# Loads of v and token weights spread over batch 0's attention in a fused attention and two-mixer kernel

## The chip, the cores and the metric

The kernel runs on one core of one Trainium2 chip. The metric is the device time of one execution in microseconds (us); the kernel before takes 465.46 us, the median of three runs (464.9 to 465.52).

The core's engines run their own instruction streams and meet at semaphores: TensorE (PE, and PEld for its weight loads), VectorE (DVE), ScalarE (ACT), GpSimd (POOL) and SyncE (SP), which here issues every transfer between HBM and the on-chip memory.

## The reference

Three stages follow one another, with batch 2, sequence 768 and width 512 (8 heads of 64):

```python
k_sum = k.reshape(B, H, nb, 32, D).max(axis=3)       # block maxima of the keys, nb = 24
v_sum = v.reshape(B, H, nb, 32, D).mean(axis=3)      # block means of the values
scores_l = where(|i - j| < 16, q @ k.T / 8, -1e9)    # a band of 31 keys
scores_s = q @ k_sum.T / 8 + log(32)                 # the 24 blocks
x = softmax([scores_l, scores_s]) @ [v, v_sum]
h = relu(x.T @ w_tok1) @ w_tok2;   u = x + h.T       # token mixing, 768 -> 256 -> 768
x = u + relu(u @ w_ch1) @ w_ch2                      # channel mixing, 512 -> 1536 -> 512
xk, xr = mu * x + (1 - mu) * x_prev                  # time shift, twice
out = sigmoid(xr @ w_r) * (relu(xk @ w_k)**2 @ w_v)
```

All inputs and the output are float32.

## The kernel before

Attention works on 12 query tiles of 128 rows, 0 to 5 for batch 0 and 6 to 11 for batch 1. For tile u the steps are named `sc` (scores: banded products of 32 queries with 64 keys, the block maxima beside them, and at the end two products that add the mask, lines 298 and 304), `max` (maximum and subtraction on DVE), `en` and `ef` (exponentials on ACT), `tr` and `tc` (transposes on PE, copied out by ACT), `pv` (products with the block means, line 348, and with v, line 355), `norm` (DVE, lines 365 and 366), then `xh` and `xl`, which split the result into a high and a low float32r part, since each large product is done as three (lines 191 to 193).

v comes in as one tile `vw` per query tile, with overlapping windows of 64 rows; `vu` (POOL, lines 247 to 250) copies the windows that overlap from neighbours. The block means of v are sums on PE: `vs b w` (line 272) multiplies window w of batch b by a constant and adds it into `vs[b]`; there are 13 windows in each batch, and the sums are complete with the last. `vd` then copies them to `vbd` on ACT (line 279), which the first `pv` needs. `km` takes the block maxima of the keys on DVE (line 254).

The token weights t1 and t2 come in three pieces each (`ld`). A piece is 64 bit words and is turned into float32 by `ca` (ACT, line 395) and `cj` (DVE, lines 407 and 408), then split by `ch` (ACT, 412) and `cl` (DVE, 415). `t1` is the first token product; `t1h` and `t1l` take its rectified high and low parts, h; `t2` is the second token product. It begins with transposes of x into the same accumulators (line 497).

The order of everything is written out by hand: `PLAN` (line 45) is a list of some 1,700 steps, and each engine runs its own instructions in that order. All transfers go out on SP in that order too. A step `gq`, `gv`, `gk`, `gx` or `gu` is a gate: SP copies one element of a tile to a scratch row (line 196), so that it, and every transfer behind it, waits until that tile has been written. 48 buffers of 4 KB a partition (`slot`) hold nearly all tiles; a new tile takes a buffer whose last reader is done.

Of the kernel before, what the change touches and what calls it, by code (L numbers as in the profile page):

```python
# [44 lines left out]
PLAN = """heat 6,vz 0,vz 1,lk 0 0,lk 0 1,km 0 0,lq 0 0 0,lk 0 2,km 0 1,lk 0 3,lq 0 0 1,km 0 2,msk,lq 0 1,cst,km 0 3,sc 0,pad 0,max 0  # L45
gq 0 0,lq 0 2,lv 0,sc 1,en 0,gq 0 1,lv 1,lv 2,ef 0,pad 1,max 1,sc 2,en 1,ef 1,gq 0 2,lv 3,lv 4,pad 2,max 2,sc 3,tr 0 0,gv 0
lv 5,ld t1 0,gv 2,ld t1 1,gv 4,ld t1 2,en 2,tc 0 0,ef 2,pad 3,max 3,tr 0 1,sc 4,tc 0 1,en 3,vs 0 0,vs 0 1,ef 3,tr 1 0,pad 4
max 4,vs 0 2,vs 0 3,tc 1 0,pad 5,vu 0,vu 1,tr 1 1,sc 5,tc 1 1,en 4,vs 0 4,vs 0 5,tr 2 0,ef 4,max 5,vs 0 6,vs 0 7,ca t1 0
tc 2 0,vu 2,vu 3,vs 0 8,vs 0 9,tr 2 1,ca t1 1,vs 0 10,tc 2 1,vs 0 11,vs 0 12,cj t1 0,tr 3 0,tr 3 1,vd 0,vu 4,vu 5,gv 5
ld t2 0,tc 3 0,pv 0,cj t1 1,tc 3 1,ch t1 0,ld t2 1,ca t1 2,cl t1 0,pv 1,norm 0,xh 0,cj t1 2,en 5,tr 4 0,ef 5,ld t2 2,xl 0  # L50
pv 2,norm 1,tc 4 0,tr 4 1,xh 1,t1 0,xl 1,pv 3,ch t1 1,norm 2,tc 4 1,mu,cl t1 1,gx 1,xh 2,norm 3,tr 5 0,gx 2,lk 1 0,t1 1,xl 2
tc 5 0,tr 5 1,ch t1 2,pv 4,tc 5 1,xh 3,gx 3,lk 1 1,cl t1 2,xl 3,pv 5,t1 2,ca t2 0,lk 1 2,norm 4,cj t2 0,ca t2 1,xh 4,ca t2 2
norm 5,xl 4,gk 1 0,lk 1 3,ch t2 0,gk 1 1,lv 6,cl t2 0,t1 3,gk 1 2,lv 7,xh 5,cj t2 1,t1 4,gk 1 3,lv 8,xl 5,ch t2 1,cj t2 2
vs 1 0,vs 1 1,t1 5,gv 6,lv 9,cl t2 1,ch t2 2,vs 1 2,om,vs 1 3,t1h 0 0,cl t2 2,gv 7,vu 6,lv 10,t1h 0 1,vs 1 4,vs 1 5,t1l 0 0
t1l 0 1,gv 8,vu 7,lv 11,km 1 0,vs 1 6,t2 0 0 0,km 1 1,gv 9,vu 8,ld c 0 0,km 1 2,t2 0 1 0,t2h 0 0 0,km 1 3,gv 10,vu 9,ld c 1 0
t2l 0 0 0,vs 1 7,vs 1 8,t2h 0 1 0,vs 1 9,gv 11,vu 10,vu 11,lq 1 0,vs 1 10,vs 1 11,t2 0 2 0,ca c 0 0,t2l 0 1 0,cj c 0 0,lq 1 1
ca c 1 0,t2 0 3 0,ch c 0 0,cj c 1 0,gu 0 1 0,lq 1 2,t2h 0 2 0,t2l 0 2 0,ch c 1 0,vs 1 12,sc 6,t2h 0 3 0,cl c 0 0,vd 1
t2l 0 3 0,t2 0 0 1,pad 6,cl c 1 0,t2 0 1 1,max 6,t2h 0 0 1,sc 7,t2h 0 1 1,en 6,sc 8,pad 7,ef 6,max 7,tr 6 0,pad 8,tr 6 1,sc 9
tc 6 0,max 8,tc 6 1,en 7,t2 0 2 1,pad 9,ef 7,max 9,tr 7 0,t2h 0 2 1,sc 10,tc 7 0,en 8,tr 7 1,pv 6,pad 10,max 10,tc 7 1,en 9
ef 8,ef 9,tr 8 0,norm 6,tr 8 1,sc 11,tc 8 0,tc 8 1,en 10,tr 9 0,pad 11,max 11,ef 10,tr 9 1,pv 7,tc 9 0,tc 9 1,xh 6,t2 0 3 1  # L60
en 11,xl 6,ef 11,norm 7,c1 0 0,t2h 0 3 1,xh 7,xl 7,tr 10 0,c1h 0 0,pv 8,tc 10 0,c1l 0 0,tr 10 1,c1 0 1,norm 8,tc 10 1,xh 8
xl 8,tr 11 0,c1h 0 1,pv 9,tc 11 0,c1l 0 1,tr 11 1,pv 10,norm 9,tc 11 1,xh 9,pv 11,norm 10,xl 9,xh 10,t1 6,norm 11,gq 1 0
ld c 0 1,gq 1 1,ld c 2 0,gq 1 2,ld c 1 1,ld c 3 0,gu 0 3 1,ld c 2 1,ld c 3 1,gx 8,ld c 4 0,ld c 5 0,ld c 4 1,gx 9,ld c 6 0
gx 10,ld c 5 1,ca c 0 1,t1 7,xl 10,cn c 0 1,ld c 7 0,ca c 2 0,cj c 0 1,ca c 3 0,t1 8,ld c 6 1,ch c 0 1,cn c 2 0,cl c 0 1,t1 9
cn c 3 0,ld c 8 0,cj c 2 0,ca c 1 1,cj c 3 0,c2 0 0 0,ch c 2 0,ld c 9 0,c2 0 0 1,ch c 3 0,cl c 2 0,cn c 1 1,c2 0 0 2,cl c 3 0
ca c 2 1,c2 0 0 3,ld c 7 1,cj c 1 1,cn c 2 1,c1 0 2,ch c 1 1,cj c 2 1,ld c 8 1,ca c 4 0,cl c 1 1,ch c 2 1,ca c 5 0,cl c 2 1
ld c 10 0,t1 10,cn c 4 0,c1h 0 2,cj c 4 0,cn c 5 0,ld c 11 0,c2 0 1 0,c1l 0 2,ch c 4 0,c2 0 1 1,cj c 5 0,ca c 3 1,cl c 4 0
c2 0 1 2,ld c 9 1,ch c 5 0,c2 0 1 3,cn c 3 1,cl c 5 0,c1 0 3,xh 11,ld c 10 1,cj c 3 1,ca c 4 1,xl 11,ch c 3 1,ld c 11 1
cn c 4 1,cl c 3 1,ca c 6 0,cj c 4 1,c2 0 2 0,c1h 0 3,wst e 1 0,c2 0 2 1,ch c 4 1,c1l 0 3,c2 0 2 2,ca c 7 0,cl c 4 1,cn c 6 0
c2 0 2 3,wst e 1 1,cn c 7 0,c1 0 4,cj c 6 0,ca c 5 1,cj c 7 0,gx 11,ch c 6 0,ch c 7 0,cl c 6 0,cn c 5 1,cl c 7 0,c2 0 3 0  # L70
ca c 6 1,cj c 5 1,wst e 1 3,c2 0 3 1,c1h 0 4,ch c 5 1,c2 0 3 2,c1l 0 4,cn c 6 1,c2 0 3 3,cl c 5 1,ca c 8 0,cj c 6 1,c1 0 5
ca c 9 0,ch c 6 1,cn c 8 0,cl c 6 1,cn c 9 0,cj c 8 0,c2 0 4 0,ca c 7 1,cj c 9 0,c1h 0 5,c2 0 4 1,ch c 8 0,c1l 0 5,t1 11
ch c 9 0,cl c 8 0,cn c 7 1,cl c 9 0,wst e 2 0,c2 0 4 2,ca c 8 1,cj c 7 1,c2 0 4 3,t1h 1 0,t1h 1 1,c1 0 6,t1l 1 0,wst e 2 1
ch c 7 1,t1l 1 1,cn c 8 1,cl c 7 1,ca c 10 0,cj c 8 1,ca c 11 0,c2 0 5 0,ch c 8 1,c2 0 5 1,c1h 0 6,cl c 8 1,cn c 10 0
c2 0 5 2,c1l 0 6,cn c 11 0,c2 0 5 3,cj c 10 0,ca c 9 1,cj c 11 0,t2 1 0 0,ch c 10 0,ch c 11 0,c1 0 7,cl c 10 0,t2h 1 0 0
cl c 11 0,cn c 9 1,ws e 2 0,ca c 10 1,wst e 2 3,cj c 9 1,cn c 10 1,ws e 2 1,ca c 11 1,t2 1 1 0,c1h 0 7,cj c 10 1,c2 0 6 0
ch c 9 1,ws e 2 2,c2 0 6 1,t2h 1 1 0,c1l 0 7,ch c 10 1,c2 0 6 2,cl c 9 1,cn c 11 1,c2 0 6 3,cl c 10 1,wh e 2 5,t2 1 2 0
wh e 2 6,cj c 11 1,wh e 2 4,wl e 2 5,c1 0 8,t2h 1 2 0,wl e 2 6,wst e 2 5,ch c 11 1,ws e 2 3,cl c 11 1,wh e 2 2,ld e 1 2
wl e 2 4,t2 1 3 0,c1h 0 8,wl e 2 2,ld e 1 3,c1l 0 8,c2 0 7 0,t2h 1 3 0,c2 0 7 1,bs 0 1 0,bs 0 1 2,c2 0 7 2,ld e 1 0,bs 0 1 1
c2 0 7 3,t2 1 0 1,bs 0 1 3,bh 0 1 0,wst e 2 6,bl 0 1 0,ca e 1 2,c1 0 9,bh 0 1 1,wst e 2 4,t2h 1 0 1,bl 0 1 1,cn e 1 2  # L80
wst e 2 2,ca e 1 3,cj e 1 2,cn e 1 3,t2 1 1 1,ca e 1 0,cj e 1 3,cn e 1 0,ws e 1 0,c2 0 8 0,cj e 1 0,t2h 1 1 1,c2 0 8 1
ws e 1 1,c2 0 8 2,ws e 1 2,c2 0 8 3,t2 1 2 1,c1h 0 9,c1l 0 9,c1 0 10,t2h 1 2 1,t2 1 3 1,c2 0 9 0,ld e 1 1,t2h 1 3 1,c2 0 9 1
c1h 0 10,bs 0 2 0,bh 0 1 5,c2 0 9 2,c1l 0 10,c2 0 9 3,bl 0 1 5,c1 0 11,ye 0 0,bs 0 2 1,ld a 0 0,ye 0 1,c2 0 10 0,c1h 0 11
c2 0 10 1,ca e 1 1,c1l 0 11,cn e 1 1,c2 0 10 2,c2 0 10 3,cj e 1 1,c2 0 11 0,ws e 1 3,ca a 0 0,c2 0 11 1,cn a 0 0,yh 0 0
c2 0 11 2,yh 0 1,c2 0 11 3,yl 0 0,p 0 1 2 0,yh 0 2,bh 0 1 6,yl 0 1,bh 0 1 4,yh 0 3,p 0 1 2 1,ye 1 0,pc 0 1 2,yl 0 2,yl 0 3
bh 0 1 2,p 0 1 2 5,pa 0 1 2 0,bh 0 1 3,ye 1 1,bl 0 1 6,wh e 1 5,gh 1 2 0,pa 0 1 2 1,p 0 1 2 6,wh e 1 6,bl 0 1 4,gl 1 2 0
p 0 1 2 4,pa 0 1 2 2,bl 0 1 2,pa 0 1 2 3,wh e 1 4,p 0 1 2 2,pa 0 1 2 4,bl 0 1 3,gh 1 2 2,pa 0 1 2 5,wh e 1 2,p 0 1 2 3
wl e 1 5,gh 1 2 3,wl e 1 6,wst e 1 5,p 0 1 1 0,pa 0 1 2 6,gl 1 2 2,gh 1 2 1,wst e 1 6,p 0 1 1 1,wl e 1 4,pc 0 1 1,gl 1 2 3
p 0 1 1 5,wl e 1 2,wst e 1 4,pa 0 1 1 0,gl 1 2 1,p 0 1 1 6,gh 1 1 0,wst e 1 2,pa 0 1 1 1,gl 1 1 0,p 0 1 1 4,ld e 0 0
pa 0 1 1 2,cj a 0 0,p 0 1 1 2,pa 0 1 1 3,wh a 0 0,ld e 0 2,pa 0 1 1 4,p 0 1 1 3,pa 0 1 1 5,gh 1 1 2,ld e 0 3,wl a 0 0  # L90
gh 1 1 3,c2 1 8 0,gl 1 1 2,c2 1 8 1,pa 0 1 1 6,ld e 0 1,c2 1 8 2,gl 1 1 3,gh 1 1 1,bs 0 2 2,c2 1 8 3,ca e 0 0,ld a 0 1
gl 1 1 1,cn e 0 0,c2 1 9 0,bs 0 2 3,ca e 0 2,c2 1 9 1,ld a 0 2,cn e 0 2,cj e 0 0,c2 1 9 2,wh e 0 0,cj e 0 2,c2 1 9 3,ca e 0 3
wst a 0 0,wl e 0 0,c2 1 10 0,cn e 0 3,c2 1 10 1,ca e 0 1,cj e 0 3,c2 1 10 2,cn e 0 1,ws e 0 0,c2 1 10 3,ca a 0 1,cj e 0 1
c2 1 11 0,cn a 0 1,ws e 0 1,c2 1 11 1,wh e 0 1,ws e 0 2,c2 1 11 2,wh e 0 5,wl e 0 1,wh e 0 6,c2 1 11 3,wl e 0 5,ca a 0 2
p 0 1 0 0,ld a 0 3,wl e 0 6,wh e 0 4,ws e 0 3,cn a 0 2,p 0 1 0 1,wl e 0 4,pc 0 1 0,cj a 0 1,wh e 0 2,cj a 0 2,p 0 1 0 5
wh e 0 3,pa 0 1 0 0,wl e 0 2,gh 1 0 0,p 0 1 0 6,pa 0 1 0 1,gl 1 0 0,p 0 1 0 4,ca a 0 3,pa 0 1 0 2,cn a 0 3,wl e 0 3,wh a 0 1
p 0 1 0 2,pa 0 1 0 3,pa 0 1 0 4,p 0 1 0 3,cj a 0 3,bh 0 2 0,pa 0 1 0 5,gh 1 0 2,ws a 0 0,wh a 0 3,c2 1 4 0,gh 1 0 3
# [800 lines left out]
```

## Time and profile before

| | |
|---|---|
| median of three runs | 465.46 us |
| profiled execution, its own time | 465.3 us |
| its span | 463.0 us |
| PE busy | 447.0 us, 97% of the span |
| DVE busy | 364.2 us, 79% |
| ACT busy | 277.1 us, 60% |
| POOL busy | 40.2 us, 9% |
| transfers | 106.27 MB, mean 230 GB/s |
| granted clock of PE | full, in every slice |

PE is busy nearly throughout. The lower shares stand in the first slices of the page, which are attention. An engine's idle time before an instruction is given in brackets in the timeline, with what ended it; "issue" means that the profile shows nothing that it waited for.

### The profile page before, as it was taken

How to read it: one execution, taken by the hardware profiler on the slowest of the kernel's cores; microseconds unless marked ns; L12 is line 12 of the kernel's file. 1: busy time of each engine (PE TensorE's matmuls, PEld its weight loads, DVE VectorE, ACT ScalarE, POOL GpSimd, SP SyncE). 2: the span in 40 equal slices, each digit the busy share in tenths (PEclk: the TensorE clock that was granted, in tenths of full speed). 3: DMA queues.
4: the chain of work that ended last, by engine and by line, in shares of the span. 5: the costliest groups of instructions: out<-in, count | busy, mean ns of one | idle time of the engine just before them, and what ended most of it. 6: DMA issues, size and time to landing. Idle time of an engine off the chain costs nothing.

```text
span 463.0 us, 10930 instructions
## 1 busy us (share of the span) xinstructions
PE 447.0 (97%) x4420; PEld 392.4 (85%) x4420; DVE 364.2 (79%) x581; ACT 277.1 (60%) x499; POOL 40.2 (9%) x110
## 2 busy tenths in 40 slices
...
GB/s 251 257 222 128 216 184 48 293 316 403 95 127 189 174 45 1 259 286 2 209 380 275 303 392 214 336 390 91 376 340 361 292 361 191 315 296 133 341 0 91
DMA packets 34803, 106.27 MB, mean 230 GB/s; under 512 B 3710, under 2 KB 10306, under 8 KB 34754
## 3 DMA queue, kind: packets, MB, share of 16 engines
...
q8 instruction: 34, 0.56, 0.5%
q14 instruction: 15, 0.12, 0.1%
...
## 4 chain that ended last, share of the span: by engine, by line
PE 81%; DVE 4%; issue 1%; ACT 0%; DVEq 0%
PE p L191 8%; PE p L192 8%; PE p L193 8%; PE acc L191 7%; PE acc L193 7%; PE acc L192 7%; PE v L193 4%; PE v L191 4%; PE v L192 4%; PE r L191 2%; PE h L193 2%; PE r L192 2%; PE h L192 2%; PE r L193 2%; PE h L191 2%; PE u L505 2%
## 5 line engine op out<-in xcount | busy, mean ns | idle before, releaser
L700 DVE TENSOR_TENSOR ev<-p,ev 128x512 f32<-128x512 f32 x84 | 56.2, 686 | 21.0 <-PE p L193 17.8
L191 PE MATMUL p<-xs,wba 128*128 128x256 f32 x168 | 47.4, 282 | 1.6 <-DVE ev L700 1.6
L191 PE MATMUL v<-wbv,k 128*128 128x256 f32 x168 | 47.1, 280 | 0.0
L192 PE MATMUL v<-wbv,k 128*128 128x256 f32 x168 | 47.1, 280 | 0.0
L193 PE MATMUL v<-wbv,k 128*128 128x256 f32 x168 | 47.1, 280 | 0.0
L192 PE MATMUL p<-xs,wba 128*128 128x256 f32 x168 | 47.0, 280 | 0.0
L193 PE MATMUL p<-xs,wba 128*128 128x256 f32 x168 | 47.0, 280 | 0.0
L191 PE MATMUL acc<-hq,wc 128*128 128x512 f32 x96 | 37.8, 394 | 0.0
L193 PE MATMUL acc<-hq,wc 128*128 128x512 f32 x96 | 37.8, 393 | 0.0
L192 PE MATMUL acc<-hq,wc 128*128 128x512 f32 x96 | 37.7, 393 | 0.0
L191 PEld LDWEIGHTS p<-xs,wba 128*128 128x128 f32 x168 | 31.6, 188 | 2.1 <-DVE ev L700 2.0
L191 PEld LDWEIGHTS v<-wbv,k 128*128 128x128 f32 x168 | 31.8, 189 | 0.1
L192 PEld LDWEIGHTS v<-wbv,k 128*128 128x128 f32 x168 | 31.8, 189 | 0.1
L193 PEld LDWEIGHTS v<-wbv,k 128*128 128x128 f32 x168 | 31.8, 189 | 0.0
L192 PEld LDWEIGHTS p<-xs,wba 128*128 128x128 f32 x168 | 31.6, 188 | 0.1
L193 PEld LDWEIGHTS p<-xs,wba 128*128 128x128 f32 x168 | 31.6, 188 | 0.0
L570 ACT ACTIVATE hq<-ev 128x512 fp32r<-128x512 f32 x24 | 14.9, 632 | 24.2 <-DVE ev L700 24.2
L693 ACT COPY ev<-p 128x512 f32<-128x512 f32 x12 | 7.0, 587 | 36.3 <-PE p L193 36.3
L191 PE MATMUL p<-xs,wae 128*128 128x256 f32 x88 | 24.8, 282 | 1.2 <-ACT wae L446 1.2
L704 ACT ACTIVATE ev<-ev 128x512 f32<-128x512 f32 x24 | 15.1, 632 | 16.8 <-DVE ev L700 16.5
L192 PE MATMUL p<-xs,wae 128*128 128x256 f32 x88 | 24.8, 282 | 0.0
L193 PE MATMUL p<-xs,wae 128*128 128x256 f32 x88 | 24.7, 281 | 0.0
...
## 6 DMA issues: line engine op xcount, KB each, us to landing
...
```

The costliest lines, as they stand in the source:

```text
L191: PE.matmul(o, lhsT=wh, rhs=xh, start=start, stop=False)
L192: PE.matmul(o, lhsT=wh, rhs=xl, start=False, stop=False)
L193: PE.matmul(o, lhsT=wl, rhs=xh, start=False, stop=stop)
L505: PE.matmul(ps[:, dst:dst + m], lhsT=h1[b, k][:, low, d], rhs=x[:, i, o:o + m], start=False, stop=low == 1 and k == 1 and pi == len(pieces ...
L570: A.activation(out=h2_block(c, d, q, 0), in_=x, func=AF.Relu)
L693: A.copy(out=block(z, c, d, 0), in_=pr[z, c, d, 0])
L700: V.tensor_tensor(out=block(z, c, d, o), in0=pr[z, c, d, p], in1=block(z, c, d, x), op=ALU.add)
L704: A.activation(out=x, in_=x, func=AF.Relu)
```

## The change

Four things are done. (1) `PLAN` is reordered over both attentions' loads: the mask goes ahead of the third key tile; the loads of v4, v5, of the t1 pieces and of the t2 pieces get gates of their own, among them a new one, `gt`, on a transposed tile `et`; in batch 1 the first two v tiles go ahead of the last two key tiles. (2) Steps of the weights' conversion (`ca`, `cj`, `ch`, `cl`) move accordingly, and two key maxima of batch 1 move back. (3) `vsum` handles two heads' groups in one matmul. (4) The transposes at the start of `t2` can be run by a step of their own, `t2x`; it is used for the first two.

```diff
+PLAN = """heat 6,vz 0,vz 1,lk 0 0,lk 0 1,km 0 0,lq 0 0 0,msk,lk 0 2,km 0 1,lk 0 3,lq 0 0 1,km 0 2,lq 0 1,cst,km 0 3,sc 0,pad 0,max 0
+gq 0 0,lq 0 2,lv 0,sc 1,en 0,gq 0 1,lv 1,lv 2,ef 0,pad 1,max 1,sc 2,en 1,ef 1,gq 0 2,lv 3,gv 0,lv 4,pad 2,max 2,sc 3,tr 0 0
...
-        for p in range(NP):
-            r, g = 64 * (p % 2), p // 2
-            PE.matmul(vs[b][r:r + 64, 0, VW * g:VW * g + VW], lhsT=x, rhs=vw[QT * b + t][:, j, VW * p:VW * p + VW],
-                      start=(w == 0 and g == 0), stop=(w == 12 and g == 1), tile_position=(0, r))
+        v = vw[QT * b + t][:, j, :].rearrange("k (g h d) -> k g h d", g=2, h=2)
+        for h in range(2):
+            o = vs[b][64 * h:64 * h + 64, 0, 0:2 * VW].rearrange("n (g d) -> n g d", g=2)
+            PE.matmul(o, lhsT=x, rhs=v[:, :, h, :], start=(w == 0), stop=(w == 12), tile_position=(0, 64 * h))
...
-    def tok2(b, dt, g):
+    def tok2_x(b, dt, g):
...
+    def tok2(b, dt, g):
+        if (b, dt, g) not in ups:
+            tok2_x(b, dt, g)
+        d = slice(P * dt, P * dt + P)
+        ps, pieces = ups[b, dt, g], W2[b][g][3]
...
+            "gk": lambda b, p: gate(kp[b, p][:, K0:K0 + 1]), "gt": lambda u: gate(et[u][:, 0, 0:1]), "vz": lambda b: G.memset(vbd[b], 0.0),
```

On SP, the first loads of the program stood like this before (`kp` are key tiles, `q` query tiles, `msk` the mask, two loads of 34 rows):

```order
L196 DMA kp0_0_96<-in_kT 128x800
L196 DMA kp0_1_99<-in_kT 128x800
L196 DMA q0_0_103<-in_qT 128x512
L196 DMA kp0_2_105<-in_kT 128x800
L196 DMA kp0_3_109<-in_kT 128x800
L196 DMA q0_0_103<-in_qT 128x512
L196 DMA msk_75<-in_mask 34x896 x2
L196 DMA q0_1_116<-in_qT 128x1024
```

They stand like this now:

```order
L196 DMA kp0_0_96<-in_kT 128x800
L196 DMA kp0_1_99<-in_kT 128x800
L196 DMA q0_0_103<-in_qT 128x512
L196 DMA msk_75<-in_mask 34x896 x2
L196 DMA kp0_2_107<-in_kT 128x800
L196 DMA kp0_3_111<-in_kT 128x800
L196 DMA q0_0_103<-in_qT 128x512
L196 DMA q0_1_116<-in_qT 128x1024
```

The mask has moved ahead of two key tiles and half a query tile; nothing else has.

On SP, from the fourth v tile of batch 0 to the second token weights, before (`gate_sb` is the target of a gate):

```order
L196 DMA vw3_252<-in_vp 128x2x260
L196 DMA vw4_254<-in_vp 128x2x260
L196 DMA gate_sb_74<-vw0_164 1x1
L196 DMA vw5_304<-in_vp 128x2x260
L196 DMA vw5_304<-in_vp 128x260
L196 DMA rawt1_0_307<-in_w1 128x512
L196 DMA gate_sb_74<-vw2_205 1x1
L196 DMA rawt1_1_310<-in_w1 128x512
L196 DMA gate_sb_74<-vw4_254 1x1
L196 DMA rawt1_2_313<-in_w1 128x512
L196 DMA gate_sb_74<-vw5_304 1x1
L196 DMA rawt2_0_541<-in_w2 128x512
```

And now, for as many rows (`et2` is the transposed tile of query tile 2):

```order
L196 DMA vw3_252<-in_vp 128x2x260
L196 DMA gate_sb_74<-vw0_164 1x1
L196 DMA vw4_255<-in_vp 128x2x260
L196 DMA gate_sb_74<-vw1_203 1x1
L196 DMA vw5_305<-in_vp 128x2x260
L196 DMA vw5_305<-in_vp 128x260
L196 DMA gate_sb_74<-vw3_252 1x1
L196 DMA rawt1_0_309<-in_w1 128x512
L196 DMA gate_sb_74<-vw5_305 1x1
L196 DMA rawt1_1_384<-in_w1 128x512
L196 DMA gate_sb_74<-et2_444 1x1
L196 DMA rawt1_2_462<-in_w1 128x512
```

There is a gate between any two loads, and each waits for a tile one or two loads back; t2's first piece then follows a gate on `et3`, its other two follow gates on x.

On DVE, around the first normalisation (L365 and L366), before:

```order
L407 TENSOR_SCALAR rawt_0_307<-rawt_0_307 128x512
L408 SCALAR_TENSOR_TENSOR rawt_0_307<-rawt_0_307 128x512
L407 TENSOR_SCALAR rawt_1_310<-rawt_1_310 128x512
L408 SCALAR_TENSOR_TENSOR rawt_1_310<-rawt_1_310 128x512
L415 TENSOR_TENSOR wt_0_584<-rawt_0_307,wt_0_584 128x512
L365 RECIPROCAL dn<-xo_544 128x8
L366 TENSOR_TENSOR xf_0_627<-xo_544,dn 128x512
```

And now:

```order
L407 TENSOR_SCALAR rawt_0_309<-rawt_0_309 128x512
L408 SCALAR_TENSOR_TENSOR rawt_0_309<-rawt_0_309 128x512
L365 RECIPROCAL dn<-xo_519 128x8
L366 TENSOR_TENSOR xf_0_597<-xo_519,dn 128x512
L415 TENSOR_TENSOR wt_0_558<-rawt_0_309,wt_0_558 128x512
L375 TENSOR_TENSOR xhl_601<-xf_0_597,xhl_601 128x512
L407 TENSOR_SCALAR rawt_1_384<-rawt_1_384 128x512
L408 SCALAR_TENSOR_TENSOR rawt_1_384<-rawt_1_384 128x512
```

Three operations that stood ahead of the first normalisation stand behind it: the join of t1's second piece and the low part of its first.

## Rows read from the trace of the kernel before

**Rows 1.** Stages: us, then busy us (instructions) of each engine, clock, DMA

```profile
0.00:66.00 66.00, 57.70 (x1258) 43.40 (x1258) 45.43 (x70) 30.71 (x61) 34.78 (x85) 1.00 0.69 220
66.00:463.00 397.00, 389.29 (x3163) 348.99 (x3162) 318.77 (x513) 246.37 (x438) 5.46 (x26) 1.00 0.63 231
```

**Rows 2.** Timeline of PE, batch 0's attention: start, us, what, [idle before, releaser]

```profile
16.33 1.07 PE L298 MATMUL sc<-kp,q 64*32 64x128 f32 x54 [0.98 <-issue]
17.33 0.28 PE L304 MATMUL sc<-msk 34*128 34x256 bf16 x2
17.54 0.88 PE L337 MATMUL et<-cst,e 128*128 128x128 f32 x6
18.35 1.16 PE L298 MATMUL sc<-kp,q 64*32 64x128 f32 x64
19.44 0.28 PE L304 MATMUL sc<-msk 34*128 34x256 bf16 x1
21.00 0.28 PE L304 MATMUL sc<-msk 34*128 34x256 bf16 x1 [1.28 <-issue]
21.21 0.69 PE L272 MATMUL vs<-vw,cst 128*64 128x65 f32 x16
...
26.60 1.15 PE L272 MATMUL vs<-vw,cst 128*64 128x65 f32 x30 [0.38 <-issue]
...
29.93 0.99 PE L348 MATMUL xo<-vbd,et 64*128 64x130 f32 x8 [0.15 <-ACT vbd L279]
...
32.59 0.32 PE L355 MATMUL xo<-vw,et 64*32 64x65 f32 x8 [0.94 <-issue]
32.84 0.72 PE L348 MATMUL xo<-vbd,et 64*128 64x130 f32 x8
```

**Rows 3.** DMA queues, 16.4 to 30 us, then 30.1 to 40 us

```profile
q1 hardware_dynamic: 2120, 4.26, 94.7%
q8 instruction: 2, 0.03, 0.9%
...
q1 hardware_dynamic: 105, 0.06, 2.0%
q8 instruction: 3, 0.05, 1.9%
```

**Rows 4.** Timeline of PE, batch 1's block means and first scores

```profile
49.53 0.69 PE L272 MATMUL vs<-vw,cst 128*64 128x65 f32 x16 [0.34 <-DMA vw<-in_vp]
...
53.47 0.45 PE L272 MATMUL vs<-vw,cst 128*64 128x65 f32 x8 [0.57 <-DMA vw<-in_vp]
...
63.57 1.15 PE L298 MATMUL sc<-kp,q 64*32 64x128 f32 x64 [0.23 <-DMA q<-in_qT]
```

**Rows 5.** Timeline of PE, the end of the first scores

```profile
10.04 0.45 PE L298 MATMUL sc<-kp,q 64*32 64x128 f32 x16 [0.52 <-issue]
10.85 0.28 PE L304 MATMUL sc<-msk 34*128 34x256 bf16 x1 [0.36 <-DMA msk<-in_mask]
12.10 0.28 PE L304 MATMUL sc<-msk 34*128 34x256 bf16 x1 [0.96 <-DMA msk<-in_mask]
```

**Rows 6.** Timeline of SP's queue: a gate on x, the first v of batch 1

```profile
40.89 0.58 SPq L196 DMA_DIRECT2D gate_sb<-xf  x1
...
45.47 0.38 SPq L196 DMA_DIRECT2D vw<-in_vp  x1
```

**Rows 7.** Timeline of DVE: key maxima, and joins of token weights

```profile
8.01 1.93 DVE L254 TENSOR_REDUCE kp<-kp 128x24 f32<-128x768 f32 x2 [1.63 <-DMA kp<-in_kT]
...
44.88 0.69 DVE L408 SCALAR_TENSOR_TENSOR rawt<-rawt 128x512 uint32<-128x512 uint32 x1
...
49.65 1.05 DVE L408 SCALAR_TENSOR_TENSOR rawt<-rawt 128x512 uint32<-128x512 uint32 x1
```

**Rows 8.** Stages: the stretch from the first normalisation to h

```profile
33.00:54.00 21.00, 20.09 (x465) 15.78 (x466) 17.87 (x34) 12.09 (x22) 5.08 (x13) 1.00 0.50 146
```

**Rows 9.** Timeline of POOL: the first copy of v in batch 1

```profile
49.54 0.61 POOL L247 COPY vw<-vw 32x520 f32<-32x520 f32 x1 [15.65 <-DMA vw<-in_vp]
```

More of the change, by code (lines that the diff above doesn't have):

```diff
@@ L41 @@
 REBIAS = 2.0 ** -112
[L45 to L97, printed above, removed]
+PLAN = """heat 6,vz 0,vz 1,lk 0 0,lk 0 1,km 0 0,lq 0 0 0,msk,lk 0 2,km 0 1,lk 0 3,lq 0 0 1,km 0 2,lq 0 1,cst,km 0 3,sc 0,pad 0,max 0
@@ new lines @@
+gq 0 0,lq 0 2,lv 0,sc 1,en 0,gq 0 1,lv 1,lv 2,ef 0,pad 1,max 1,sc 2,en 1,ef 1,gq 0 2,lv 3,gv 0,lv 4,pad 2,max 2,sc 3,tr 0 0
+gv 1,lv 5,gv 3,ld t1 0,en 2,tc 0 0,ef 2,pad 3,max 3,tr 0 1,sc 4,tc 0 1,en 3,vs 0 0,vs 0 1,ef 3,tr 1 0,pad 4,max 4,vs 0 2
+vs 0 3,tc 1 0,gv 5,ld t1 1,pad 5,vu 0,vu 1,tr 1 1,sc 5,tc 1 1,en 4,vs 0 4,vs 0 5,tr 2 0,ef 4,max 5,vs 0 6,vs 0 7,ca t1 0
+tc 2 0,gt 2,ld t1 2,vu 2,vu 3,vs 0 8,vs 0 9,tr 2 1,vs 0 10,tc 2 1,vs 0 11,vs 0 12,cj t1 0,tr 3 0,tr 3 1,vd 0,vu 4,vu 5,tc 3 0
+gt 3,ld t2 0,pv 0,tc 3 1,ca t1 1,ch t1 0,pv 1,norm 0,xh 0,cl t1 0,xl 0,cj t1 1,ca t1 2,gx 0,ld t2 1,en 5,tr 4 0,ef 5,pv 2
@@ new lines @@
+norm 1,tc 4 0,tr 4 1,xh 1,xl 1,cj t1 2,pv 3,ch t1 1,norm 2,tc 4 1,mu,t1 0,gx 1,ld t2 2,xh 2,norm 3,tr 5 0,cl t1 1,gx 2,lk 1 0
+lk 1 1,t1 1,xl 2,tc 5 0,tr 5 1,ch t1 2,pv 4,tc 5 1,xh 3,gx 3,lv 6,lv 7,cl t1 2,xl 3,pv 5,t1 2,ca t2 0,gk 1 0,lk 1 2,norm 4
+cj t2 0,ca t2 1,xh 4,gk 1 1,lv 8,ca t2 2,norm 5,xl 4,ch t2 0,gv 6,lk 1 3,cl t2 0,t1 3,gv 7,lv 9,xh 5,xl 5,t1 4,cj t2 1,gk 1 2
+lv 10,ch t2 1,cj t2 2,vs 1 0,vs 1 1,t1 5,gv 8,lv 11,cl t2 1,ch t2 2,vs 1 2,om,vs 1 3,t1h 0 0,cl t2 2,vu 6,t1h 0 1,vs 1 4
@@ new lines @@
+vs 1 5,t2x 0 0 0,t2x 0 1 0,t1l 0 0,t1l 0 1,vu 7,km 1 0,vs 1 6,t2 0 0 0,km 1 1,gv 9,vu 8,ld c 0 0,t2 0 1 0,t2h 0 0 0,gv 10
+vu 9,ld c 1 0,t2l 0 0 0,km 1 2,vs 1 7,vs 1 8,t2h 0 1 0,vs 1 9,gv 11,vu 10,vu 11,lq 1 0,vs 1 10,vs 1 11,t2 0 2 0,ca c 0 0
+t2l 0 1 0,km 1 3,cj c 0 0,lq 1 1,ca c 1 0,t2 0 3 0,ch c 0 0,cj c 1 0,gu 0 1 0,lq 1 2,t2h 0 2 0,t2l 0 2 0,ch c 1 0,vs 1 12
+sc 6,t2h 0 3 0,cl c 0 0,vd 1,t2l 0 3 0,t2 0 0 1,pad 6,cl c 1 0,t2 0 1 1,max 6,t2h 0 0 1,sc 7,t2h 0 1 1,en 6,sc 8,pad 7,ef 6
+max 7,tr 6 0,pad 8,tr 6 1,sc 9,tc 6 0,max 8,tc 6 1,en 7,t2 0 2 1,pad 9,ef 7,max 9,tr 7 0,t2h 0 2 1,sc 10,tc 7 0,en 8,tr 7 1
@@ new lines @@
+pv 6,pad 10,max 10,tc 7 1,en 9,ef 8,ef 9,tr 8 0,norm 6,tr 8 1,sc 11,tc 8 0,tc 8 1,en 10,tr 9 0,pad 11,max 11,ef 10,tr 9 1
+pv 7,tc 9 0,tc 9 1,xh 6,t2 0 3 1,en 11,xl 6,ef 11,norm 7,c1 0 0,t2h 0 3 1,xh 7,xl 7,tr 10 0,c1h 0 0,pv 8,tc 10 0,c1l 0 0
+tr 10 1,c1 0 1,norm 8,tc 10 1,xh 8,xl 8,tr 11 0,c1h 0 1,pv 9,tc 11 0,c1l 0 1,tr 11 1,pv 10,norm 9,tc 11 1,xh 9,pv 11,norm 10
+xl 9,xh 10,t1 6,norm 11,gq 1 0,ld c 0 1,gq 1 1,ld c 2 0,gq 1 2,ld c 1 1,ld c 3 0,gu 0 3 1,ld c 2 1,ld c 3 1,gx 8,ld c 4 0
+ld c 5 0,ld c 4 1,gx 9,ld c 6 0,gx 10,ld c 5 1,ca c 0 1,t1 7,xl 10,cn c 0 1,ld c 7 0,ca c 2 0,cj c 0 1,ca c 3 0,t1 8,ld c 6 1
```

36 lines of the change are left out of this document (34 added, 2 removed).

## The prediction

> **What bounds the kernel now.** I read first how busy TensorE is before and after 66 us, since every edit of the change lies ahead of that point. [rows 1]: in the first 66 us PE works 57.70 us and idles 8.3; in the 397 us behind them it works 389.29, and the granted clock is 1.00 in both, the 2.4 GHz level. So from 66 us on the kernel is one chain of matmuls, and whatever moves the point at which PE enters it moves the end. Next I read what ended PE's idle time in the first part, in order of time. Three kinds of gap are to be seen.
>
> First, gaps "issue", at which no engine and no transfer is named: PE stands 0.98 us before 16.33, 1.28 before 21.00, 0.38 before 26.60 and 0.94 before 32.59 [rows 2], 3.58 us in all. Between the first two stand 54+2+6+64+1 = 127 matmuls, each with its weight load: 254 instructions; the next two stretches, counted in the same way, hold 127 and 126. So the gap returns every 256 instructions, less one or two. The queue named "instruction" moves packets of 0.56 MB/34, some 16 KB. It carries 2 of them in 16.4 to 30 us, while the data queue fills 94.7% of the 16 engines, and 3 in 30.1 to 40 us, with the data queue at 2.0% [rows 3]. In the quiet stretch no such gap appears behind 32.59, though PE uses a block there in some 4 us; in the busy one two blocks used in about 5 us still ended in gaps. I read the gaps as waits for PE's own code, whose packets stand behind loads.
>
> Second, in batch 1 PE waits 0.34 and 0.57 us for v and 0.23 for q [rows 4]. Third, at the start the fourth key product begins at 10.04, and the two mask products wait 0.36 and 0.96 us for the two mask loads, begun 1.25 us apart [rows 5].
>
> **The change part by part**, against the profiled execution: span 463.0, its own time 465.3, which is 0.16 under the median of the three runs shown (465.46).
>
> *Loads spread out.* Up to v3 nothing changes on SP but the mask, so the first gap (0.98) stays. From v4 on each load follows a one-element gate on an earlier one; t1's last piece and all of t2 wait for attention results. Their six pieces (128x512 words of 8 bytes, 3.1 MB) stand in the full queue of [rows 3]; now they come in turns up to the second and third normalisation. The second gap's packet starts with v3 and v4 in flight: I give it back a third, 0.4. The third and fourth lie where the queue will be nearly empty: 0.38 + 0.94 = 1.32. Sum -1.7. Bounds: 0 if the gaps have another cause; -3.6 if all four go. PE is in order there, and what is late next is the block-mean copy to ScalarE ahead of the first product with v, for which PE already waits 0.15 us before 29.93 [rows 2].
>
> *Block means merged.* 26 windows (13 in each batch) of four matmuls of 65 columns become two of 130. A matmul shows as two records: 16 take 0.69 us (at 21.21, [rows 2]), 0.345 a window. The nearest 130-column row, with 128 columns of weights against 64 here, takes 0.72 for 8: a window would be 0.36, +0.015. The other end is half of 0.345, if a record cost the same at twice the width: -0.17. So 26 windows give +0.4 to -4.5. Score records (128 columns, 32 of weights, eight tiles at a time) take 1.16/64 = 18 ns (at 18.35, [rows 2]); fitting one cost per moving column and one per weight column to this row and the 65-column row gives 0.31 a window, -0.9. I take -0.7, between that and the 130-column row, nearer to the first. It also takes 104 instructions out of each batch, which moves the block ends and is in the bounds.
>
> *Batch 1's v.* v6 and v7 now stand directly behind the gate that SP starts at 40.89, ahead of the last two key tiles; before, v6 went out at 45.47 [rows 6]. It is over 3 us earlier, and those behind it by less as SP's gates run on; so the waits for v and q, 0.34+0.57+0.23 = 1.14, go: -1.1. What is late next is VectorE, below. Two sets of transposes are taken ahead of one window there: the same matmuls run on PE either way, so I cost them at 0.
>
> *Mask ahead of the third key tile.* Both mask waits go, -1.3, if keys 2 and 3 arrive as now. But the second mask load (34x896 of 2 bytes, 61 KB) comes 1.25 us behind the first, 49 GB/s [rows 5], against a mean of 230 in the span: it doesn't use the width of the queue. Key tile 2 is taken by VectorE at 8.01 on its landing [rows 7]; if the piece of it that shares the mask's path waits out both masks, 2.5 us, the fourth key product goes from 10.04 to 12.54, both mask products then follow it at once, the second at some 13.0 instead of 12.10: +0.9. I take +0.4, nearer to the bad end, since the row shows the narrow path at work. The first gate waits for the q piece behind them, so the third q tile and v0 go out later too; that is hidden, since v0 is first summed at 21.21 [rows 2].
>
> The Trainium skill has a rule that speaks against this edit (DMA: Bandwidth & Descriptors, "Why a DMA increments its semaphore by 16 and not by 1"): a transfer runs on the largest number of engines up to 16 that divides its slowest dimension, and on the lowest-numbered ones. By it 34 rows would go on two engines, the same for both masks; the trace's 49 GB/s for one, one behind the other, agrees. By it the term would be +0.9 and the time 463.1.
>
> *Conversions moved.* One t1 piece's two shift-and-join steps and the first low part move from before the first normalisation to behind it. At 0.69 us each [rows 7], that is 2.1 us into a stretch in which VectorE works 17.87 of 21.0 us [rows 8]: 3.1 idle us cover it. But the POOL copies of v start some 4 us earlier too, and beside their first one the same join took 1.05 instead of 0.69 [rows 7, 9]. With two t2 conversions beside them that is at most 4 x 0.36 = 1.4; I take +0.3, the part that 3.1 - 2.1 = 1.0 us of slack doesn't hide. Without cover all 2.1 + 1.4 would count.
>
> Sum: -1.7 - 0.7 - 1.1 + 0.4 + 0.3 = -2.8: 465.3 - 2.8 = 462.5, and with the offset of the runs 462.6.
>
> **Rivals.** (a) *The gaps stay.* They may belong to a block's size and not to the loads: they come every 256 instructions, whatever runs. Then -0.7 - 1.1 + 0.7 = -1.1: 464.4. Against it stands the quiet stretch, where PE takes block after block behind 32.59 without such a gap [rows 3]. The Trainium skill says of this (Runtime: NRT & Kernel Launch, "Instruction fetch mechanics") that code comes in blocks of 256 instructions on the sequencer's own queue and that crossing a boundary is mostly hidden. By it loads would not decide the gaps, and 464.4 would be the time; the four gaps of [rows 2] differ from "hidden".
>
> (b) *The gain is given back.* Batch 1's attention takes PE's filler work in a fixed order, and its softmax runs on VectorE. If PE meets it early and waits there, or if the first gate's delay goes through to q and v, the end stays: 465.4. For it: VectorE works 17.87 of 21 us just ahead. Against: 389.29 of 397 us busy on PE [rows 1] leaves waits that move along with PE.
>
> (c) *Slower: VectorE becomes the bound between the first normalisation and the h of tok1.* Slack is 3.1 us; moved in are 2.1, and 1.4 by the POOL copies: 0.4 over. If the mask costs its 0.9 and the gaps don't shrink, the stretch begins 0.9 late and ends 1.3 late, and neither merged means nor early v count, since PE waits for h there: 466.7. It decides once the first product with block means starts no earlier than now, 29.93 us [rows 2]. Against it: three of the four gaps lie ahead of that product.
>
> **How the numbers follow.** Forecast 0.60, its own range 461.0 to 463.8 (the mask at its good end, 1.7 less; or the mask at +0.9 and no gain from the means, 1.2 more); (a) 0.19; (b) 0.12; (c) 0.09. A change under 0.2%, 0.93 us, can't be told from none: the border is 464.5. Faster: 0.60 and half of (a), which lies at the border: 0.69. Same: half of (a) and (b), 0.22. Slower: (c), 0.09. The range of 8 in 10 goes from 461.0 through (a) and (b) to 465.6; it leaves out (c) and some 0.05 below.
>
> **What would show it.** Right: after the first, PE's "issue" gaps ahead of the first normalisation are each under 0.6 us; the queue's share falls well under 94.7% behind 22 us; block-mean records number half, at about 78 ns each; PE waits for no v or q in batch 1; mask products wait for no load, while VectorE's third key maximum starts 1 to 2.5 us after 8.01; batch 1's first scores start near 60.8 instead of 63.57, and the same 2.8 us stand at the end. Wrong: gaps of a microsecond with an empty queue (a), the early scores but the old end (b), PE waiting for h or for a weight's low part before 54 us (c).

## Result and profile after

The changed kernel takes 467.99 us (median of 20 runs, 465.06 to 471.51), the kernel before 465.35 (20 runs beside them); the ratio is 1.006, 95% interval 1.0042 to 1.0079. It is 2.6 us slower where 2.8 us less were forecast, and above the range. Its runs also lie further apart: 6.5 us from lowest to highest, against 2.5. The profiled execution took 468.1 us, span 466.3. First its stages, to be read against [rows 1] (us, then busy us and instructions of PE, PEld, DVE, ACT and POOL, then PE's granted clock as a share of full speed, DMA share, GB/s):

```profile
0.00:66.00 66.00, 59.72 (x1157) 43.65 (x1158) 47.96 (x70) 30.46 (x62) 39.09 (x89) 0.97 0.71 220
66.00:466.30 400.30, 390.32 (x3161) 349.50 (x3160) 318.24 (x512) 246.27 (x438) 3.47 (x22) 1.00 0.63 229
10.00:20.00 10.00, 7.78 (x281) 5.84 (x287) 8.03 (x9) 2.69 (x6) 1.14 (x3) 0.83 0.60 184
90.00:100.00 10.00, 7.57 (x228) 6.05 (x228) 5.19 (x10) 4.99 (x10) 0.00 (x0) 0.93 0.88 268
100.00:110.00 10.00, 10.00 (x40) 7.99 (x40) 6.47 (x10) 7.54 (x14) 0.00 (x0) 0.90 1.02 404
```

The loss lies behind 66 us: that part is 3.3 us longer with 1.0 us more of PE work. One slice holds it: in 90 to 100 us PE stands 2.43 us, and there and behind it the clock is below full. Now PE's timeline, the answers to [rows 2, 4, 5], with the place of the loss:

```profile
11.68 0.45 PE L298 MATMUL sc<-kp,q 64*32 64x128 f32 x16 [1.80 <-DVE kp L254]
12.67 0.45 PE L298 MATMUL sc<-kp,q 64*32 64x128 f32 x16 [0.54 <-issue]
13.06 0.28 PE L304 MATMUL sc<-msk 34*128 34x256 bf16 x2
...
32.80 0.45 PE L355 MATMUL xo<-vw,et 64*32 64x65 f32 x28 [0.46 <-issue]
...
38.01 0.74 PE L355 MATMUL xo<-vw,et 64*32 64x65 f32 x50 [1.45 <-POOL kp L226]
...
63.44 1.16 PE L298 MATMUL sc<-kp,q 64*32 64x128 f32 x64
...
92.42 0.86 PE L355 MATMUL xo<-vw,et 64*32 64x65 f32 x64
93.22 0.72 PE L348 MATMUL xo<-vbd,et 64*128 64x130 f32 x8
93.86 0.84 PE L355 MATMUL xo<-vw,et 64*32 64x65 f32 x63
97.14 0.21 PE L355 MATMUL xo<-vw,et 64*32 64x65 f32 x1 [2.43 <-issue]
97.28 0.50 PE L191 MATMUL t<-xhl,wt 128*128 128x512 f32 x1
...
98.55 0.54 PE L193 MATMUL t<-xhl,wt 128*128 128x512 f32 x1
98.89 0.63 PE L191 MATMUL t<-xhl,wt 128*128 128x512 f32 x1
```

Batch 1's first scores start at 63.44 instead of 63.57: in this execution next to nothing is won by then. (Executions differ there by a microsecond: the quiet form below, whose instructions are the same up to 86 us, starts them at 62.34.) Ahead of 97.14 PE stands for 2.43 us, one matmul short of the end of batch 1's last product with v, and the profile names nothing that it waits for. The nine products from 98.55 to 102.19 then come 0.40 us apart where full speed gives 0.23: 1.6 us. Gap and clock together are 4.0 us. The kernel before does the same products without a gap:

```profile
92.61 0.86 PE L355 MATMUL xo<-vw,et 64*32 64x65 f32 x64
93.40 0.72 PE L348 MATMUL xo<-vbd,et 64*128 64x130 f32 x8
94.05 0.86 PE L355 MATMUL xo<-vw,et 64*32 64x65 f32 x64
94.84 0.50 PE L191 MATMUL t<-xhl,wt 128*128 128x512 f32 x1
```

Why there? A stretch without gaps can be counted in blocks, from one gap to the next. First the kernel before, from its last gap of [rows 2] on; then the changed one, from the gap at 38.01 to that at 97.14:

```profile
32.59:92.88 60.29, 59.10 (x1400) 48.52 (x1400) 45.47 (x73) 32.92 (x68) 20.19 (x47) 1.00 0.54 168
```

```profile
38.01:97.14 59.13, 56.48 (x1271) 45.71 (x1272) 45.23 (x69) 32.66 (x66) 21.19 (x40) 1.00 0.63 202
```

A matmul and its weight load are two instructions, and the trace has a few semaphore instructions of PE beside them. 1271 matmuls with their loads and 17 semaphore instructions are 2559, ten blocks of 256 less one: the gap at 97.14 is a block's end. 1400 with their loads and 16 are 2816, eleven blocks: before, a block ended near 92.88, inside the last but one product with v. The merged means take four matmuls with their weight loads out of each window, eight instructions, so 104 in each batch and 208 up to here; the end now falls behind the 63+8+57 matmuls from 92.5 to 94.5 us, which take 2.0 us.

Counted in this way, all 42 gaps "issue" of over 0.15 us between 14 and 112 us, in the traces of all fourteen kernels of this document, stand at a multiple of 256 from one another, to within two instructions. So do four gaps to which the profile gives another name; the 1.45 at 38.01 is one.

The packet with the next code (queue q8) came late: it starts at 94.86, 2.35 us into the block ahead, which began at 92.51. Queues of the changed kernel in 92.5 to 94.8 us, then 94.8 to 95.2 (packets, MB, share):

```profile
q1 hardware_dynamic: 221, 0.79, 92.2%
...
q1 hardware_dynamic: 30, 0.10, 79.1%
q8 instruction: 1, 0.02, 15.2%
```

### The profile page after: what moved, and what is told of

Read it like the earlier page. It is cut to its first block, busy times and chain, and to the rows that moved or that the text cites. A ratio compares the mean times of both kernels' runs of the same rounds, so it can differ in the third digit from the quotient of the medians.

```text
span 466.3 us, 10724 instructions
## 1 busy us (share of the span) xinstructions
PE 450.0 (97%) x4316; PEld 393.1 (84%) x4316; DVE 366.2 (79%) x581; ACT 276.7 (59%) x499; POOL 42.6 (9%) x110
## 4 chain that ended last, share of the span: by engine, by line
PE 83%; DVE 6%; POOL 4%; DMA 3%; issue 2%; SPq 1%; ACT 0%; DVEq 0%; POOLq 0%
PE p L191 8%; PE p L192 8%; PE p L193 7%; PE acc L191 7%; PE acc L193 7%; PE acc L192 7%; PE v L191 4%; PE v L192 4%; PE v L193 4%; PE u L511 4%; PE r L191 2%; PE r L193 2%; PE h L193 2%; PE h L191 2%; PE r L192 2%; PE h L192 2%
```

## Experiments

Theory A: the merging moved a block's end behind PE's densest stretch, and the code behind it came late; the half clock follows from the stop. Rival B: the loads or the mask are at fault, and the merging doesn't matter. Theory M: the mask's new place costs time by itself. Each kernel was compared with the kernel before on its own chip; all numbers are medians.

**Means as four matmuls again**, in the changed kernel; **means merged alone**, in the kernel before (the reverse of the edit shown):

```diff
-        v = vw[QT * b + t][:, j, :].rearrange("k (g h d) -> k g h d", g=2, h=2)
-        for h in range(2):
-            o = vs[b][64 * h:64 * h + 64, 0, 0:2 * VW].rearrange("n (g d) -> n g d", g=2)
-            PE.matmul(o, lhsT=x, rhs=v[:, :, h, :], start=(w == 0), stop=(w == 12), tile_position=(0, 64 * h))
+        for p in range(NP):
+            r, g = 64 * (p % 2), p // 2
+            PE.matmul(vs[b][r:r + 64, 0, VW * g:VW * g + VW], lhsT=x, rhs=vw[QT * b + t][:, j, VW * p:VW * p + VW],
+                      start=(w == 0 and g == 0), stop=(w == 12 and g == 1), tile_position=(0, r))
```

> The changed kernel with the block means as four matmuls per window again: PE's instruction count is the old one (208 more). Theory A (a PE code block now ends just behind the densest stretch of batch 1's attention, so its successor is late): the 2.43 us issue gap at 94.7 is gone, the rows t<-xhl behind it stay at 0.23 us pitch, and the time falls by 2.5 to 4 us, to 464 to 465.5. Theory B (the loss comes from the loads or the mask, the merging has nothing to do with it): the gap near 95 stays, and the time is 468 to 469.

463.16 us against 465.34, ratio 0.996 (0.994 to 0.9979): 4.8 us below the changed kernel, more than the 2.5 to 4 expected. Its stage of 90 to 100 us:

```profile
90.00:100.00 10.00, 10.00 (x231) 8.19 (x209) 7.29 (x15) 7.54 (x14) 0.00 (x0) 1.00 0.85 291
```

> The kernel before with nothing but the merged block means. Theory A: an issue gap of 1.5 us or more appears between 92 and 97 us that the kernel before does not have, with a lower granted clock behind it; the time is 467 to 469. Theory B: no such gap, the windows become 0.01 to 0.03 us shorter each, and the time is 464.7 to 465.4.

470.18 us, ratio 1.01 (1.007 to 1.013): the merging alone costs 4.8 us, more than the 2 to 4 expected. The same place in its timeline:

```profile
95.54 0.86 PE L355 MATMUL xo<-vw,et 64*32 64x65 f32 x64
98.64 0.47 PE L191 MATMUL t<-xhl,wt 128*128 128x512 f32 x1 [2.24 <-DVE rawc L408]
...
99.64 0.63 PE L192 MATMUL t<-xhl,wt 128*128 128x512 f32 x1
```

The gap has another name here (a DVE step that happened to end in it), but it is the same stop, one matmul later, with half speed behind it. In this execution, whose span is 5.3 us longer, stop and half speed are 3.9; 1.5 stand ahead of them, where PE waits 0.64 and 2.21 us for v in batch 1 (0.34 and 0.57 in [rows 4]), and no run tells whether the merging makes those waits. A holds; B, that the merging doesn't matter, falls.

**Only the place.** In the changed kernel three of the six warming matmuls are replaced by 110 tiny ones, so that the block ends of batch 1 lie where they were:

```diff
-PLAN = """heat 6,vz 0,vz 1, ...
+PLAN = """heat 3,tiny 110,vz 0,vz 1, ...
...
+    def tiny(n):
+        w = psum("warm")
+        for _ in range(n):
+            PE.matmul(w[0:32, 0:8], lhsT=warm[:, 0:32], rhs=warm[:, 0:8], start=True, stop=True)
```

> The changed kernel, means merged, with half of the warming matmuls at the start replaced by 110 tiny ones (32x32 weights, 8 columns, results unused), so that PE's instruction count up to batch 1 is that of the kernel before again. Theory A, that only the place of the block's end counts: no gap of over 1 us near 95, and 464 to 466 (up to 1 us for the changed start). Theory B: the gap near 95 stays with the merged windows, 468.

464.17 us, ratio 0.9987 (0.9969 to 1.0004); no gap near 95, though the means are merged. It keeps two gaps in batch 0:

```profile
33.59 0.30 PE L360 MATMUL xo<-vw,et 64*32 64x65 f32 x4 [1.38 <-issue]
...
38.79 0.44 PE L360 MATMUL xo<-vw,et 64*32 64x65 f32 x26 [1.28 <-issue]
```

The reverse is the sharpest test. Into the kernel with four matmuls and the masks back (462.21, below), 24 tiny matmuls are put at the start: 48 instructions, and since 208 + 48 = 256, a block's end then falls where the merging had put it. Eight tiny ones are the control.

```diff
-PLAN = """heat 6,vz 0,vz 1, ...
+PLAN = """heat 6,tiny 24,vz 0,vz 1, ...
```

> The unmerged kernel with the masks back (462.21), with 24 tiny matmuls (48 instructions, some 0.6 us) added at the very start and nothing else. It puts a block's end at the same product of batch 1 as in the changed kernel, 48 instructions earlier than before; by the trace of that kernel the 256 instructions ahead of it take 2.03 us. Theory A: a gap of 1.8 to 2.9 us near 93 to 96, half the clock behind it in most runs, 465 to 469. If merging or the 130-column form matters, not the place: no such gap, 462.2 to 463.0.

465.82 us, ratio 1.0014 (0.9995 to 1.0034). Its timeline there:

```profile
91.11 0.72 PE L353 MATMUL xo<-vbd,et 64*128 64x130 f32 x8
91.75 0.84 PE L360 MATMUL xo<-vw,et 64*32 64x65 f32 x63
95.09 0.21 PE L360 MATMUL xo<-vw,et 64*32 64x65 f32 x1 [2.49 <-issue]
95.23 0.79 PE L191 MATMUL t<-xhl,wt 128*128 128x512 f32 x1
95.81 0.63 PE L192 MATMUL t<-xhl,wt 128*128 128x512 f32 x1
```

> The same with 8 tiny matmuls (16 instructions, 0.2 us): the block's end in batch 1 then closes 256 instructions that take 5.4 us. Theory A: no gap over 0.3 us between 88 and 100, 462.0 to 463.0. If tiny matmuls at the start cost time by themselves: between 462.2 and the 24's time, in proportion.

462.33 us, ratio 0.9941 (0.9926 to 0.9956), with no gap there; the 24 cost 3.5 us more. With no merged matmul, the stop returns at the same matmul: the place is the cause.

**Half of the merging**, batch 0's alone:

```diff
+        if b:
+            for p in range(NP):
+                r, g = 64 * (p % 2), p // 2
+                PE.matmul(vs[b][r:r + 64, 0, VW * g:VW * g + VW], lhsT=x, rhs=vw[QT * b + t][:, j, VW * p:VW * p + VW],
+                          start=(w == 0 and g == 0), stop=(w == 12 and g == 1), tile_position=(0, r))
+            return
```

> The changed kernel with batch 0's means merged and batch 1's as four matmuls: 104 instructions fewer than unmerged in place of 208. In the unmerged kernel the 256 instructions that end 104 behind its block end at 91.77 take 3.10 us; those that end 208 behind it take 2.03 us, and there the changed kernel waited 2.65. Theory A: a gap of 1.3 to 1.9 us near 94 to 95, smaller than the changed kernel's, and 464.8 to 467.3. If the merging itself (the 130-column form) costs the time in batch 1: no gap, 463 to 464. If in batch 0 or in any merged window: 467.5 to 468.5.

470.05 us, ratio 1.0104 (1.0071 to 1.0137): too high for every theory. The stop is where A put it, 53 matmuls before the end, but as long as the changed kernel's:

```profile
98.28 1.10 PE L361 MATMUL xo<-vw,et 64*32 64x65 f32 x53 [2.47 <-issue]
```

I expected 1.3 to 1.9 us, on the thought that the code takes a fixed time to come. It took 5.8 us from the start of the block ahead (92.48, by counting back 256 instructions) to the restart, against 4.6 (92.51 to 97.14) in the changed kernel. So the time isn't fixed. The part that differs lies ahead of the q8 packet: it starts 3.53 us into the block here (at 96.01) and 2.35 in the changed kernel, and PE restarts 2.27 and 2.28 us behind it. What holds the packet back was the next question.

**A quiet queue.** In the changed kernel two gates are drawn ahead of four loads of channel weights:

```diff
-... gu 0 3 1,ld c 2 1,ld c 3 1,gx 8,ld c 4 0
-ld c 5 0,ld c 4 1,gx 9,ld c 6 0,gx 10,ld c 5 1, ...
+... gu 0 3 1,ld c 2 1,ld c 3 1,gx 8,gx 9
+gx 10,ld c 4 0,ld c 5 0,ld c 4 1,ld c 6 0,ld c 5 1, ...
```

> The changed kernel with three of the channel weights' loads held back behind two gates (from 88.1 us to behind 94), so that few transfers are in flight while PE waits near 95; its block end stays where it is. If the loads in flight lengthen the wait for the block: the 2.43 us gap shrinks to 0.9 to 1.8 (the 2.03 us that the 256 instructions take against 3.46 us from block to block in the quiet stretch behind 32.59 of the kernel before), the clock holds, and the time is 465 to 467 unless the held weights are late. If only the place counts: 2.2 to 2.7, 467 to 468.5.

(Four loads, not three, are held behind the gates.) 463.76 us, ratio 0.9973 (0.9958 to 0.9988): 4.0 us less than the changed kernel (each against its kernel before), with not one product changed. Its stage of 91 to 94 us, the q8 packet in 91 to 91.5, and PE at the same block's end:

```profile
91.00:94.00 3.00, 2.75 (x143) 2.12 (x141) 1.77 (x4) 1.35 (x4) 0.00 (x0) 1.00 0.02 5
```

```profile
q8 instruction: 1, 0.02, 11.5%
```

```profile
92.69 0.84 PE L355 MATMUL xo<-vw,et 64*32 64x65 f32 x63
93.79 0.21 PE L355 MATMUL xo<-vw,et 64*32 64x65 f32 x1 [0.25 <-issue]
```

The packet goes as the block ahead of it begins (91.36 us, the block at 91.33), not 2.35 us into it, the stop is 0.25 instead of 2.43, and the clock stays at 1.00. From the packet's start to the restart it is 2.43 us, hardly other than the 2.28 with loads: loads in flight put off the start of the packet. Gap and time both came out below what I expected: loads in flight make nearly the whole stop, and the place decides whether it is felt.

**The mask.** Moved alone in the kernel before (the reverse of the edit shown), then put back in the changed kernel, in its four-matmul form and in the quiet form:

```diff
 ... lk 0 0,lk 0 1,km 0 0,lq 0 0 0,
-msk,lk 0 2,km 0 1,lk 0 3,lq 0 0 1,km 0 2,
+lk 0 2,km 0 1,lk 0 3,lq 0 0 1,km 0 2,msk,
 lq 0 1,cst,km 0 3,sc 0, ...
```

> The kernel before with nothing but the mask loads put ahead of the third key tile. Theory M (the masks' narrow path delays key tiles 2 and 3 by some 2.5 us, PE idles there and the granted clock falls in the first scores): VectorE's third key maximum starts at 10 us or later, the first scores end 0.9 later, the scores behind them run at 1.2 GHz, sc3 starts 2 us or more later, and the time is 465.8 to 467.5. Rival (the later fetch gaps swallow all of it, or the keys come as before): 464.1 to 465.4.

465.41 us against 465.34, ratio 0.9995 (0.9972 to 1.0019): the rival. M's first half is there: DVE's third key maximum starts at 10.05 (changed kernel: 10.62) instead of 8.01 [rows 7], and the next scores run at half speed (1.96 us for the 64 records that take 1.16 in [rows 2]):

```profile
10.05 1.95 DVE L254 TENSOR_REDUCE kp<-kp 128x24 f32<-128x768 f32 x2 [3.77 <-DMA kp<-in_kT]
```

```profile
13.02 1.96 PE L298 MATMUL sc<-kp,q 64*32 64x128 f32 x64
```

But the gaps "issue" behind it shrink to 1.03, 0.24 and 0.33 us, 1.6 in all for 3.58, and the wait for q is gone; that for v is not (0.94 against 0.91). Batch 1's first scores start at 63.30 (63.57 before).

> The changed kernel with the masks at their old place; merged means and spread loads stay. Theory A (the block's end decides): the issue gap of 2 us or more near 95 stays, with the half clock behind it; 467 to 469. If the mask's move is what costs the changed kernel its 2.6 us: no loss against the kernel before, 464.5 to 465.5. The granted clock of 10 to 20 us is 1.00 again under either.

467.21 us, ratio 1.0051 (1.0031 to 1.0071). The gap near 95 is 1.86, a little under the 2 expected: still there, as A says. The clock of 10 to 20 us is 1.00 again.

> Only the spread loads and the two transposes taken ahead are left of the change: four matmuls per window and the masks at their old place. If the mask's move costs time of its own (PE idles 1.7 us ahead of the third key product and runs the next scores at half clock): 0.5 to 2 us under the 463.16 of the four-matmul kernel with the mask moved, 461.2 to 462.7. If what it loses early is taken back in the waits for code and v behind it, as in the kernel before (465.41 against 465.34): 462.9 to 463.6.

462.21 us, ratio 0.9937 (0.9912 to 0.9963), the lowest median of all, and in the range of the first case (the four pairs are set side by side below). Its first scores behind the masks, its gaps "issue" in batch 0 and batch 1's first scores:

```profile
12.23 1.96 PE L298 MATMUL sc<-kp,q 64*32 64x128 f32 x64
...
20.93 0.28 PE L304 MATMUL sc<-msk 34*128 34x256 bf16 x1 [1.03 <-issue]
...
34.87 0.45 PE L355 MATMUL xo<-vw,et 64*32 64x65 f32 x28 [0.54 <-issue]
...
61.46 1.15 PE L298 MATMUL sc<-kp,q 64*32 64x128 f32 x64 [0.19 <-DMA q<-in_qT]
```

The half speed in the first scores is here with the masks back (1.96 us for the 64, granted clock 0.83 in 10 to 20 us; 0.66 in the next form), so it isn't shown that the mask's move makes it.

> The changed kernel with both repairs: the held loads of the quiet version (463.76) and the masks at their old place; means merged, loads of v and token weights spread. If the mask's move costs some 0.5 us beside any of the versions, as between the two pairs with and without it (463.16 and 462.21; 467.99 and 467.21): 462.8 to 463.5, and the gap near 94 under 0.8. If the quiet version's short gap was one lucky profile: a gap of 1.4 or more, 464.5 to 467. If merging pays once the block's end is covered: under 461.8.

463.12 us, ratio 0.9968 (0.9945 to 0.9992); the stop near 94 is under 0.2 us, so the quiet form's profile was no luck. Against each run's own kernel before, the mask's move is worth 0.07, 0.5, 0.65 and 0.4 us in the four pairs, all inside the intervals: some 0.4 us at most likely, not shown from zero. And the merging, once its block's end in batch 1 is covered, still shows no gain: 463.12 against 462.21 in the unmerged form, whose channel weights' loads aren't held back, with intervals that overlap. Two stops of 1.2 us remain at other block ends in batch 0.

**The clock at the start.** One more warming matmul in the four-matmul form:

```diff
-PLAN = """heat 6,vz 0,vz 1, ...
+PLAN = """heat 7,vz 0,vz 1, ...
```

> The four-matmul form of the changed kernel (463.16) with one more warming matmul at the start (seven, 1.3 us each, for six), so that PE hardly idles ahead of the third key product; the block ends move by 4 instructions. If the clock's fall in 10 to 20 us costs time: the granted clock there is 0.95 or more, the fourth q tile's scores start 1 us or more earlier, and the time is 461.8 to 462.8. If waits behind it swallow that: 463.0 to 463.5 with the clock up.

463.03 us, ratio 0.9958 (0.994 to 0.9976), as without it (463.16). The clock of 10 to 20 us rises to 0.95 (0.83 without), and the next wait for code takes the gain:

```profile
17.79 1.08 PE L298 MATMUL sc<-kp,q 64*32 64x128 f32 x56 [1.69 <-issue]
...
19.02 1.51 PE L337 MATMUL et<-cst,e 128*128 128x128 f32 x6
20.46 1.96 PE L298 MATMUL sc<-kp,q 64*32 64x128 f32 x64
```

The half speed isn't gone either. It comes behind that wait: the six transposes take 1.51 us for the 0.88 of [rows 2], the 64 scores 1.96 for 1.16. So this run doesn't tell what half speed at the start costs.

## Why the prediction was wrong

**The step that failed** is in *Block means merged*: "It also takes 104 instructions out of each batch, which moves the block ends and is in the bounds." It was not: the bounds, +0.4 to -4.5, came from the duration of the matmuls alone. Those were about right. The group of the block means before and after:

```profile
L272 PE MATMUL vs<-vw,cst 128*64 128x65 f32 x208 | 8.6, 226 | 1.3 <-DMA vw<-in_vp 0.9 <-issue 0.4
```

```profile
L273 PE MATMUL vs<-vw,cst 128*64 128x130 f32 x104 | 8.0, 283 | 0.0
```

0.6 us less busy, 0.7 forecast. But the whole edit, alone, measured +4.8, and in the changed kernel's profile the stop at 97.14 and the half speed behind it are 4.0. The other terms summed to -2.1 (-1.7 - 1.1 + 0.4 + 0.3); the changed kernel without the merging came out at -2.18. So the forecast was off by one term, and by its sign.

**Why I missed it.** I had the period of 256 instructions and the tie to the loads, and used both only for the four gaps I saw. "In the quiet stretch no such gap appears" I took as clearing everything behind 32.59; and from 389.29 of 397 us busy I read that behind 66 us PE is one chain that only slides. A block's end that costs nothing now leaves no row. Counted on from the last gap, as above, it can be placed all the same (the prediction's "less one or two" are PE's semaphore instructions), and the dense 2.0 us at batch 1's end with the channel weights in flight (DMA 0.80 in that slice before) stood in the trace.

**Rival (a)** said that the gaps belong to the block, not the loads. Both are needed: the same block's end costs 2.43 us with loads and 0.25 without; with loads it costs nothing where the block takes longer to run (5.3 us up to 92.88 in the kernel before). The Trainium skill (Runtime: NRT & Kernel Launch, "Instruction fetch mechanics") has the next block fetched while the present one runs and the crossing mostly hidden. The quiet form agrees (packet at the block's start, 0.25 us); with loads in the queue the trace differs, by 2.43 us.

**Loads, -1.7 by shorter gaps; batch 1's v, -1.1.** Alone (masks back, four matmuls) they and the conversions measured -2.83 against -2.5. The waits for v and q of [rows 4] are gone but for 0.19, and batch 1's first scores are 2.1 us early; with the mask moved, the four-matmul form still waits 0.84 for v. The size is in part luck. The gaps "issue" fell by 2.0 us, from 3.58 to 1.03 + 0.54, but the first is gone, which was to stay, and the fourth has a successor at the next block's end. And one reason was wrong: "where the queue will be nearly empty" is false, since the spread loads now fill it. Their gates reach further back than I wrote ahead of the prediction: v4 waits for v0 and v5 for v1, so three v tiles may still be on their way behind the one that is waited for. The changed kernel's queue in 30.1 to 40 us, against 2.0% in [rows 3]:

```profile
q1 hardware_dynamic: 721, 2.08, 67.8%
```

Gaps remain there (0.46 and 1.45 in the changed kernel, 0.54 in the unmerged one), and which is felt depends again on where the blocks end.

**Mask, +0.4.** Right in size, as far as the runs can tell. The place was read rightly: mask products wait for no load, and the first scores end at 13.06 + 0.28 = 13.34 instead of 12.38, the +0.9 of the bad end. Behind that the fourth q tile's scores start 2.4 us late (17.30 for 14.91), since the clock falls as well, which no term held (and which two forms with the masks back show too); the waits behind took it back.

**Rivals (b) and (c).** (b) named batch 1's softmax; the gain was given back, but to PE's code. (c) forecast slower by VectorE; VectorE decides nothing here: with the same loads and conversions the unmerged kernel is faster.

**What would show it.** Means at half the records, waits for v gone, gaps "issue" under 0.6 us ahead of the first normalisation: seen. The queue's share in 22 to 30 us fell to 63.6% (96.4 before). First scores near 60.8: 63.44 in the changed kernel, 61.46 in the best. Of the signs of being wrong, "gaps of a microsecond with an empty queue" came otherwise: with a full queue, at a place that I had not named.
